# Eight attention units in four lanes ahead of two chunks that run together, and another chain that converts the weights

## The chip, the cores and the metric

The kernel runs on one core of a Trainium2 chip. The time is device microseconds of one execution; of the kernel before there are three: 1543.84, 1540.35 and 1537.54 us, median 1540.35 us. The engines are TensorE (PE, its weight loads PEld), VectorE (DVE), ScalarE (ACT), GpSimd (POOL) and SyncE (SP), which here only issues DMA transfers. Each engine runs its own instructions in the order in which they stand in its program.

## The reference, cut to what is computed

```
def sm_attn(qq, kk, vv):                      # scale = 1/8
    s = scale * qq @ kk.T
    a = exp(s - max(s));  a = a / (sum(a) + 1e-09)
    return a @ vv
# 8 batches, 8 heads, 576 positions, head width 64, 32 packed queries p
p_packed = sm_attn(p, k, v)
x = sm_attn(q, p_packed, p_packed)            # as (8, 576, 512)
# first mixer
x_prev = x moved by one position
xk = mu_k*x + (1-mu_k)*x_prev;  xr = mu_r*x + (1-mu_r)*x_prev
x2 = sigmoid(xr @ w_r) * (relu(xk @ w_k)**2 @ w_v)      # 512 -> 1024 -> 512
# second mixer
u = x2 + (U, V of rank 32 over the positions)
out = u + relu(u @ w_ch1) @ w_ch2                       # 512 -> 2048 -> 512
```

The weights come as 64-bit floats, q, k, v and p as 32-bit floats.

## The kernel before

**Units and chunks.** Attention is cut into 16 units: batch pair b (0 to 3) times head pair j (0 to 3), unit u = 4b + j. `attention_steps` computes one: it transposes k on PE, forms the packed scores, takes exp, transposes q and the weights, forms the packed output `pp`, the second scores, a second softmax (`a2`, `s2`: 20 groups of 32 columns) and the output `xo`, which one DMA writes to `x_d`. Every product goes through a PSUM tile `psat`, and ACT or DVE copies it out. A unit loads three inputs `kin`, `qin`, `vin` of 576 KB each.

The first mixer works on 12 chunks of 384 positions, three to a batch pair. Chunk n reads x of all four units of its batch pair, mixes it (`mix`, tiles `xr` and `xk`, each in two halves hi and lo), then `r_block` (three of 12 products, PSUM `psr`), `k_block` (eight of 12 products, `psk`, then relu, square and split to `kk`), `v_block` (eight of 9 products into three accumulators `psv`), `x2_out` and `xu_block`. The second mixer (`psc`) begins when all chunks are done.

**Weights.** `Cast.run` loads 128x512 64-bit words into `st` and makes from the two 32-bit halves of each a hi and a lo tile (fp32r). The four tiles of w_r and the left half of w_k (`wk_0`) are needed for a chunk's start, the right half (`wk_1`) from its fifth `k_block` on, the eight of w_v (`wv`) in its `v_block`s. The first eight conversions stand between the first loads (`FIRST`), the other twelve behind them. The 34 conversions of V, w_ch1 and w_ch2 follow during the chunks. `st` has 2 buffers, and the scratch tiles `a` and `m` have 2 each.

**Order of the work.** `Plan` collects all operations with a class and a sequence number, and `emit` walks through them with its own costs and writes the engines' programs; a `copy` goes to ACT or DVE as it falls out there. So the order within each engine is fixed when the program is built. At the start units 0 to 3 run together in four lanes (buffer sets A, B, C, D: `AX_`), each `LAG` = 3 steps behind the one before, with all eight PSUM banks. Lane A has eight big buffers and loads unit 4's inputs while unit 0 runs; B, C and D have four each, and their memory then becomes `w1b` (wk_1 and wv) and the chunk pools (`open_c`). After that chunk 0 begins, and units 4 to 15 follow one at a time in lane A with two PSUM banks, their steps lying between the chunks' products: units 4 to 7 from chunk 0 on, since chunk 3 needs them, 8 to 11 from chunk 3, 12 to 15 from chunk 6.

## Time and profile before

| | |
|---|---|
| median of three runs | 1540.35 us (1537.54 to 1543.84) |
| profiled execution | span 1538.1 us from its first to its last instruction; the profile names no other time of it |
| busy share of the span | PE 97%, PEld 85%, DVE 63%, ACT 46%, POOL 18% |
| mean granted TensorE clock | 0.984 of 2.4 GHz |
| chain that ended last | PE 91%, DMA 3%, DVE 2%, SP 2%, ACT 2% |

The profiled execution's span lies 2.25 us under the median of the runs, and within their spread. A busy PE is not a PE at its peak: a product at half clock, or one that waits inside the pipeline, counts as busy too. In the chain that ended last a run of products on PE shows how long they take when nothing is in their way.

### The profile page before, as it was taken

What the parts mean: (1) busy time and instruction counts of PE and PEld (TensorE: products, weight loads), DVE (VectorE), ACT (ScalarE), POOL (GpSimd) and SP (SyncE); (2) the same over time, 40 slices, a digit from 0 to 9 for tenths busy, and PEclk for the clock granted to TensorE, in tenths of its full rate; (3) what the DMA queues carried; (4) which work ended last, traced back from release to release, by engine and by line L of the source; (5) the groups of instructions that cost most, each with busy time, mean ns of one, the idle gap of its engine ahead of it and who ended that gap; (6) DMA issues with size and microseconds to landing.
All of it is one profiled execution on the core that took longest, in us unless ns stands there. A gap on an engine that the chain in (4) does not pass through costs nothing.

```text
span 1538.1 us, 25958 instructions
## 1 busy us (share of the span) xinstructions
PE 1491.3 (97%) x9460; PEld 1303.1 (85%) x9460; DVE 962.4 (63%) x2221; ACT 707.1 (46%) x1635; POOL 270.3 (18%) x522
## 2 busy tenths in 40 slices
PE   6779899999999999999999999999999999999998
PEld 4657688888888888888899999999999899999997
DVE  6888877888778886875745454444535354444533
ACT  5777657656756765665522232323222232322221
POOL 0000000000000000001233333333333333333331
PEclk9779999999999999999999999999999999999999
DMA  9865455555555444656877767686866767676763
GB/s 232 206 156 147 122 141 159 155 165 153 160 149 154 139 152 144 223 206 209 263 178 217 190 172 221 166 239 160 230 165 188 203 166 225 161 219 157 205 170 101
DMA packets 202174, 275.67 MB, mean 179 GB/s; under 512 B 68928, under 2 KB 95872, under 8 KB 202048
## 3 DMA queue, kind: packets, MB, share of 16 engines
q0 software_dynamic: 72576, 132.15, 33.0%
q1 hardware_dynamic: 129472, 141.87, 31.1%
q8 instruction: 76, 1.25, 0.3%
q14 instruction: 50, 0.41, 0.1%
HBM read 221.45 MB, written 52.50 MB: 178 GB/s over the span
## 4 chain that ended last, share of the span: by engine, by line
PE 91%; DMA 3%; DVE 2%; SPq 2%; ACT 2%; issue 1%; DVEq 0%
PE psc L197 49%; PE psk L197 13%; PE psv L197 13%; PE psr L197 6%; PE psat L197 4%; PE psat L209 2%; SPq L312 2%; PE psu L197 1%; PE psh L197 1%; PE pst L209 1%; DMA vin<-in_v_dram 1%; DMA s<-w_d 1%; DMA st<-in_moe_w_k_dram 0%; ACT a L230 0%; DMA kin<-in_k_dram 0%
## 5 line engine op out<-in xcount | busy, mean ns | idle before, releaser
L197 PE MATMUL psc<-w,hid 128*128 128x512 f32 x1728 | 446.2, 393 | 1.3 <-ACT xu L281 1.3
L197 PEld LDWEIGHTS psc<-ob,wb 128*128 128x128 f32 x3024 | 406.9, 190 | 26.7
L197 PE MATMUL psc<-ob,wb 128*128 128x256 f32 x3024 | 420.8, 283 | 0.0
L312 POOL DMA_DIRECT2D wb<-ws_d x504 | 267.2, 531 | 593.6 <-PE psc L197 498.6
L197 PEld LDWEIGHTS psc<-w,hid 128*128 128x128 f32 x1728 | 306.2, 189 | 52.0 <-ACT xu L281 1.6
L197 PE MATMUL psk<-xk,wk 128*128 128x384 f32 x1152 | 232.3, 344 | 3.4 <-ACT sq L230 2.4
L197 PE MATMUL psv<-wv,kk 128*128 128x512 f32 x864 | 231.7, 402 | 3.7 <-DVE wv L251 2.2
L197 PEld LDWEIGHTS psk<-xk,wk 128*128 128x128 f32 x1152 | 202.4, 189 | 13.9 <-ACT sq L230 3.3
L251 DVE TENSOR_TENSOR tmp<-tmp,psc 128x256 f32<-128x256 f32 x288 | 120.5, 419 | 143.4 <-PE psc L197 142.2
L230 ACT ACTIVATE hid<-tmp 128x256 fp32r<-128x256 f32 x216 | 85.2, 417 | 262.9 <-DVE tmp L251 262.7
L197 PEld LDWEIGHTS psv<-wv,kk 128*128 128x128 f32 x864 | 157.4, 189 | 37.9 <-DVE wv L251 4.2
L266 DVE SCALAR_TENSOR_TENSOR hid<-psc,hid 128x256 fp32r<-128x256 f32 x72 | 30.5, 424 | 188.3 <-ACT hid L230 188.3
L197 PE MATMUL psr<-wr,xr 128*128 128x512 f32 x432 | 114.7, 408 | 6.9 <-ACT r L281 2.7
L281 ACT ACTIVATE tmp<-psc 128x256 f32<-128x256 f32 x144 | 54.6, 379 | 126.5 <-PE psc L197 126.5
L197 PEld LDWEIGHTS psr<-wr,xr 128*128 128x128 f32 x432 | 80.7, 193 | 26.5 <-ACT r L281 3.8
L266 DVE SCALAR_TENSOR_TENSOR hid<-tmp,hid 128x256 fp32r<-128x256 f32 x216 | 86.3, 422 | 23.6 <-ACT hid L230 19.1
L304 POOL MEMSET x<- 128x8 f32 x4 | 0.5, 134 | 563.6 <-DVE m L263 385.9
L251 DVE TENSOR_TENSOR kk<-sq,kk 128x384 fp32r<-128x384 f32 x96 | 52.6, 552 | 41.3 <-ACT kk L281 41.1
L230 ACT ACTIVATE sq<-psk 128x384 f32<-128x384 f32 x96 | 46.4, 487 | 67.8 <-PE psk L197 66.9
L230 ACT ACTIVATE hid<-psc 128x256 fp32r<-128x256 f32 x72 | 27.5, 382 | 102.6 <-PE psc L197 102.6
L263 DVE SCALAR_TENSOR_TENSOR m<-x,mu_t,m 128x384 f32<-128x384 f32 x96 | 57.8, 611 | 6.6 <-ACT m L230 6.4
L230 ACT ACTIVATE m<-x,om_t 128x384 f32<-128x384 f32 x96 | 57.3, 610 | 7.5 <-DVE xk L251 3.8
(152 smaller groups left out, 1670.4 us busy)
## 6 DMA issues: line engine op xcount, KB each, us to landing
wb<-ws_d POOLq DMA_DIRECT2D x504, 256.0 KB, 3.1
st<-in_moe_w_ch_dram SPq DMA_DIRECT2D x32, 512.0 KB, 4.3
ws_d<-wb SPq DMA_DIRECT2D x56, 256.0 KB, 3.2
...
```

Source lines behind the costliest of these rows:

```text
L197: self.nc.tensor.matmul(o, l, r, start=start, stop=stop, **k)
L209: self.nc.tensor.transpose(out.get(), in_.get(), ident.get())
L230: self.nc.scalar.activation(o, in_.get(), func, **k)
L251: return self.elem(engs, lambda e, o, x, y: e.tensor_tensor(out=o, in0=x, in1=y, op=op), out, [a, b], self.TT, cls)
L263: ("dve",), lambda e, o, x, y, z: e.scalar_tensor_tensor(out=o, in0=x, scalar=z, in1=y, op0=op0, op1=op1), out, [a, b, s], {"dve": (1.042, ...
L266: ("dve",), lambda e, o, x, y: e.scalar_tensor_tensor(out=o, in0=x, scalar=s, in1=y, op0=op0, op1=op1), out, [a, b], self.TT, cls)
L281: self.nc.scalar.activation(o, i, AF.Copy)
L304: (self.nc.gpsimd if eng == "pool" else self.nc.vector).memset(o, 0.0)
L312: (self.nc.sync if eng == "sp" else self.nc.gpsimd).dma_start(out=o, in_=i)
```

## The change

Units 0 to 7 run first, two after another in each of the four lanes (`ORDER`). In lanes B, C and D the second unit's buffers are claimed, and its loads issued, only where the first one makes `xo`. Once unit 3 is done attention leaves PSUM banks 3 and 4 to `psr` and `psk`. Chunks 0 and 1 then go together: their mixes and `r_block`s are in class 0, as attention is, their `k_block`s and `v_block`s alternate, and chunk 1 has three more accumulators, in banks 5 to 7. Lane A's eight big buffers serve meanwhile as `rs` (six r tiles), `x_lead` and `kk_lead` (named `prs`). Units 8 to 11 are given with chunk 2, units 12 to 15 with chunk 5. The twelve late conversions write to `w1b`, which opens when all units of lanes B, C and D are done. `st` and the `m` pool get a third buffer, unit 7 is computed in the plain way of units 0 to 6 (`NPLAIN`).

The conversion chain has one ACT operation less (the copy `m`), and on DVE seven operations as before: four tensor_scalar and three scalar_tensor_tensor, where two tensor_scalar, two scalar_tensor_tensor and three tensor_tensor stood; the copy to hi stays, on ACT or DVE. The second softmax of a unit is taken over all 20 groups at once from exp on.

```diff
     LAG = 3
+    LANES, ORDER = "BCD", (0, 1, 2, 3, 0, 1, 2, 3)
+    EARLY = ()
+    LATER = "v0 v1 v2 k0 k1 k2 k3 v3 v4 v5 v6 v7"
+    NLEAD = 2 * NJ
     FIRST = "k0 p0 q0 w0 k1 v0 w1 q1 v1 w2 k2 q2 w3 v2 k3 w4 q3 v3 w5 w6 w7"
-    NPLAIN = 7
+    NPLAIN = 8
...
-        if u_next is not None:
+        def claim():
             A.kin[u_next], A.qin[u_next], A.vin[u_next] = [A.tile_in(n) for n in ("kin", "qin", "vin")]
+
+        early = u_next is not None and not A.first
+        if early:
+            claim()
...
-        if u_next is not None:
+        if early:
             A.load_k(u_next, A.after)
 
...
-        plan.reduce(st[:, 0:1], sps[0][:, 0:320], ALU.max)
-        plan.reduce(st[:, 1:2], sps[1][:, 0:256], ALU.max)
-        plan.tt(st[:, 2:3], st[:, 0:1], st[:, 1:2], ALU.max)
-        plan.ts(st[:, 3:4], st[:, 2:3], -SCALE, None, mul)
+        s0, s1 = st.at(0), st.at(1)
+        plan.reduce(s0[:, 0:1], sps[0][:, 0:320], ALU.max)
+        plan.reduce(s0[:, 1:2], sps[1][:, 0:256], ALU.max)
+        plan.ts(s0[:, 3:4], s0[:, 0:1], s0[:, 1:2], -SCALE, ALU.max, mul)
...
-            av, s = a2.on(g)[:, g0:g1, :], s2.at(g)
-            bc = [P, g1 - g0, NP]
-            plan.reduce(s[:, 0, g0:g1], sv, ALU.max)
-            plan.tt(av, sv, s[:, 0, g0:g1].unsqueeze(2).to_broadcast(bc), sub)
-            plan.act(av, av, AF.Exp, scale=SCALE)
-            plan.reduce(s[:, 1, g0:g1], av, add)
-            plan.ts(s[:, 2, g0:g1], s[:, 1, g0:g1], 1e-9, None, add)
-            plan.recip(s[:, 3, g0:g1], s[:, 2, g0:g1])
-            plan.tt(av, av, s[:, 3, g0:g1].unsqueeze(2).to_broadcast(bc), mul)
-
...
+            plan.reduce(s2.at(g)[:, 0, g0:g1], sv, ALU.max)
+            plan.tt(a2.on(g)[:, g0:g1, :], sv,
+                    s2.at(g)[:, 0, g0:g1].unsqueeze(2).to_broadcast([P, g1 - g0, NP]), sub)
+        plan.act(a2, a2, AF.Exp, scale=SCALE)
+        plan.reduce(s2[:, 1, :], a2, add)
+        plan.ts(s2[:, 2, :], s2[:, 1, :], 1e-9, None, add)
+        plan.recip(s2[:, 3, :], s2[:, 2, :])
+        plan.tt(a2, a2, s2[:, 3, :].unsqueeze(2).to_broadcast([P, 20, NP]), mul)
+
+        a2f = a2g = a2.rearrange("p g k -> p (g k)")
...
+        if u_next is not None and A.first:
+            claim()
+            A.load_k(u_next)
+            A.load_q(u_next)
+            A.load_v(u_next)
...
-            top = h = sv[:, :, 1].bitcast(F32)
+            top, hb, low = sv[:, :, 1].bitcast(F32), sv[:, :, 1], sv[:, :, 0]
+            ab, mb = a.bitcast(I32), m.bitcast(I32)
             plan.act(a, top, AF.Abs)
-            plan.stt(h, a, 1.125 * 2.0 ** -15, top, ALU.is_ge, mul)
-            plan.act(m, sv[:, :, 0].bitcast(U32), AF.Copy, scale=2.0 ** -52)
-            hb, ab = sv[:, :, 1], a.bitcast(I32)
-            plan.ts(ab, hb, 3, 0x3FFFFFF8, ALU.logical_shift_left, ALU.bitwise_and)
-            plan.stt(ab, hb, -0x40000000, ab, ALU.bitwise_and, ALU.bitwise_or)
-            plan.ts(hb, ab, -0x800000, None, ALU.bitwise_and)
-            plan.tt(m, m, h, mul)
-            plan.tt(m, m, a, add)
+            plan.ts(a, a, 1.125 * 2.0 ** -15, None, ALU.max)
             if parts is None:
+                plan.ts(mb, ab, 3, 0x3FFFFFF8, ALU.logical_shift_left, ALU.bitwise_and)
...
+                plan.stt(m, low.bitcast(U32), 2.0 ** -52, top, mul, mul)
+                plan.tt(m, m, a, add)
                 put(whole[1])
             else:
-                split(*parts, m)
+                hi, lo = parts
+                plan.ts(mb, ab, 3, 0x3FFFF000, ALU.logical_shift_left, ALU.bitwise_and)
+                plan.stt(mb, hb, -0x40000000, mb, ALU.bitwise_and, ALU.bitwise_or)
+                plan.copy(hi, m)
+                plan.ts(hb, mb, -0x800000, None, ALU.bitwise_and)
+                plan.ts(ab, ab, 0x1FF, None, ALU.bitwise_and)
+                plan.stt(a, ab, 2.0 ** 32, low.bitcast(U32), mul, add)
+                plan.stt(lo, a, 2.0 ** -52, top, mul, mul)
...
-                                  for n, b in (("xin", 1), ("mix", 6), ("m", 2))]
+                                  for n, b in (("xin", 1), ("mix", 6), ("m", 3))]
...
-    AX_ = [A0] + [Bufs(es_st, n, "left", 4, True) for n in "BCD"]
+    AX_ = [A0] + [Bufs(es_st, n, "left", 4, True) for n in LANES]
+    lane = [AX_[i] for i in ORDER]
+    nxt = {}
+    for u in range(NLEAD):
+        nxt[u] = next((w for w in range(u + 1, NLEAD) if lane[w] is lane[u]), None)
...
-    steps = [attention_steps(AX_[u], u, NJ if u == 0 else None) for u in range(NJ)]
+    steps = [attention_steps(lane[u], u, nxt[u]) for u in range(NLEAD)]
+    prev = {w: u for u, w in nxt.items()}
     step = 0
     while any(s is not None for s in steps):
+        if steps[NJ - 1] is None:
+            att_banks[0] = banks[0:3] + banks[5:8]
         for i, s in enumerate(steps):
-            if s is not None and step >= i * LAG and next(s, False) is False:
+            if s is None or step < i * LAG or (i in prev and steps[prev[i]] is not None):
+                continue
+            if next(s, False) is False:
                 steps[i] = None
         step += 1
     att_banks[0] = ps_a
     A0.after = ()
+    rs = [plan.tile(A0.big_p, [P, 1152], F32, "big", parts=(0, 1), name="rs") for _ in range(3)]
+    r_lead = [t.at(h)[:, h * 512:(h + 1) * 512] for t in rs for h in range(2)]
+    pairs = [plan.tile(A0.big_p, [P, 1152], F32R, "big", parts=(0, 1), name="prs")[:, 0:2 * CW]
+             .rearrange("p (a c) -> p a c", a=2) for _ in range(5)]
+    x_lead, kk_lead = pairs[0:2], pairs[2:5]
+    xin_lead = [t.vt.bitcast(F32)[:, 0:1024].rearrange("p (j c) -> p j c", j=2) for t in kk_lead[1:3]]
 
...
-        cast_v(m)
+    late_casts = LATER.split()
+    for _ in EARLY:
+        cast_late(late_casts.pop(0))
+    plan.open(cpools + [w1b], [pl for A in AX_[1:] for pl in A.pools], open_c)
+    for t in late_casts:
+        cast_late(t)
...
+        if n == 1:
+            for h, t in enumerate(xin_lead):
+                plan.dma(t, x_d[b].rearrange("(j p) n -> p j n", p=P)[:, 2 * h:2 * h + 2, c * CW - P:c * CW + CW], cls=0)
+            xin[n] = lambda j: xin_lead[j // 2][:, j % 2]
+            return
...
-        s = plan.tile(hid_p, [P, CW], F32, "s", name="sq")
+        s = plan.tile(m_p, [P, CW], F32, "m", name="sq")
         plan.act(s, ps[:, 0:CW], AF.Relu)
         plan.square(s, s)
-        kk = plan.tile(kk_p, [P, 2, CW], F32R, "kk", parts=(0, 1))
+        if n < 2 and (2 * m + n) % 6 < 3:
+            kk = kk_lead[(2 * m + n) % 3]
+        else:
+            kk = plan.tile(kk_p, [P, 2, CW], F32R, "kk", parts=(0, 1))
...
-            vps[:] = [plan.bank(ps_v, "psv") for _ in range(3)]
+            vps[n] = [plan.bank(banks[5 + t:6 + t] if n == 1 else ps_v, "psv", n != 1) for t in range(3)]
...
-    CAST0, NPER = 1, 5
+    CAST0, NPER = 2, 5
...
+        return [(n, t, x2_out(n, t)) for t in range(3)]
+
+    plan.cls = 0
+    evac = []
+    for n in range(2):
+        load_x(n)
+        for j in range(NJ):
+            mix(n, 1, j, x_lead[j - 2] if n == 1 and j >= 2 else None)
+        for t in range(3):
+            evac.append(r_block(n, t))
+        for j in range(NJ):
+            mix(n, 0, j, xm[n, 1, j] if n == 1 else None)
+    for n in range(2):
+        sigmoid(n, evac + [x_last[0]])
+    plan.cls = 1
+    load_x(2)
+    for m in range(MK):
+        for n in range(2):
+            k_block(n, m)
+        if m >= 2:
+            for n in range(2):
+                v_block(n, m - 2)
+    for n in range(2):
+        v_block(n, MK - 2)
     for j in range(NJ):
-        mix(0, 1, j)
+        mix(2, 1, j)
     x2s = []
-    for n in range(len(chunks)):
+    A0.load_k(NLEAD)
+    A0.load_q(NLEAD)
+    A0.load_v(NLEAD)
+    for n in range(2, len(chunks)):
         b, c = chunks[n]
-        if c == 0 and b + 1 < NBP:
...
+        if c == 2 and b + 2 < NBP:
             plan.cls = 1 if b == 0 else 0
-            for u in range((b + 1) * NJ, (b + 2) * NJ):
+            for u in range((b + 2) * NJ, (b + 3) * NJ):
                 attention(A0, u, u + 1 if u + 1 < NU else None)
...
-            if t == 0 and n > 0:
+            if t == 0 and n == 2:
+                for n0 in range(2):
+                    v_block(n0, MK - 1)
+                x2s = [(n0, t0, x2_out(n0, t0)) for t0 in range(3) for n0 in range(2)]
+            elif t == 0:
                 x2s = finish(n - 1)
...
-                if n > 0 and m in (1, 2, 3):
-                    xu_block(n - 1, m - 1, x2s.pop(0))
+                if m > 0 and x2s:
+                    xu_block(*x2s.pop(0))
```

How instructions move is shown at three places. First the lead on PE, where `psat<-ident,kin` begins a unit. In the kernel before, unit 4's transposes of k stand ahead of the end of units 2 and 3, and the first `psr` (chunk 0) behind:

```order
L209 MATMUL psat<-ident,kin 64x128 x2
L209 MATMUL psat<-ident,pbd 128x128
L197 MATMUL psat<-th,ppz 128x320 x2
L197 MATMUL psat<-th,ppz 128x256 x2
L197 MATMUL psat<-kh,pT 32x256 x4
L197 MATMUL psat<-kt,pT 32x64 x4
L197 MATMUL psat<-kh,pT 32x256 x4
L209 MATMUL psat<-ident,a_916 128x128 x5
L197 MATMUL psr<-wr_177,xr 128x512 x2
L197 MATMUL psat<-th,ppz 128x320 x2
L197 MATMUL psat<-th,ppz 128x256 x2
L197 MATMUL psr<-wr_177,xr 128x512
```

In the change the same stretch holds the transposes of units 6 and 7 (`kin`) and chunk 0's first `psr`:

```order
L209 MATMUL psat<-ident,kin 64x128 x2
L209 MATMUL psat<-ident,pbd 128x128
L197 MATMUL psat<-vin,at 32x64 x20
L209 MATMUL psat<-ident,kin 128x128 x4
L197 MATMUL psr<-wr_181,xr 128x512 x2
L209 MATMUL psat<-ident,qin 128x128
L209 MATMUL psat<-ident,pp 128x128
L209 MATMUL psat<-ident,qin 128x128 x2
L197 MATMUL psr<-wr_181,xr 128x512
L209 MATMUL psat<-ident,a_160 128x128 x4
L209 MATMUL psat<-ident,kin 128x128 x4
L197 MATMUL psr<-wr_181,xr 128x512 x3
```

So the first products of the chunks stand where four more units have begun, and each next piece of `psr` has pieces of units 4 to 7 ahead of it.

Second, SP's queue at the end of the lead. Before, the loads of the late weights (`st<-in_moe_w_k`, `st<-in_moe_w_v`) stand between the loads and stores of units 0 to 5:

```order
L312 DMA st<-in_moe_w_k_dram 128x1024
L312 DMA x<-x_d_65 128x4x512
L312 DMA st<-in_moe_w_k_dram 128x1024
L312 DMA st<-in_moe_w_v_dram 128x1024
L312 DMA x_d_66<-xo 128x1152
L312 DMA st<-in_moe_w_v_dram 128x1024
L312 DMA kin<-in_k_dram 128x2x256 x2
L312 DMA kin<-in_k_dram 64x2x64 x2
L312 DMA st<-in_moe_w_v_dram 128x1024 x2
```

In the change three of them stand ahead of unit 2's store, and the other nine behind the stores of units 4 to 7 (`x_d_66<-xo`):

```order
L316 DMA x<-x_d_65 128x2x63
L316 DMA prs<-x_d_65 128x2x512
L316 DMA x_d_66<-xo 128x1152
L316 DMA x<-x_d_65 128x4x512
L316 DMA prs<-x_d_65 128x2x512
L316 DMA x_d_66<-xo 128x1152 x3
L316 DMA st<-in_moe_w_k_dram 128x1024 x4
L316 DMA st<-in_moe_w_v_dram 128x1024 x5
L316 DMA st<-in_moe_U_dram 64x576 x2
L316 DMA x<-x_d_66 128x384
L316 DMA x<-x_d_66 128x2x63
```

Third, PE where the two chunks run together. Before, chunk 0 has one `psk` block after another and a `psv` block (`wv`) as soon as its weights are there:

```order
L197 MATMUL psk<-xk,wk_0_184 128x384 x6
L197 MATMUL psk<-xk,wk_0_181 128x384 x3
L197 MATMUL psk<-xk,wk_0_182 128x384 x3
L197 MATMUL psk<-xk,wk_0_183 128x384 x3
L197 MATMUL psk<-xk,wk_0_184 128x384 x2
L209 MATMUL psat<-ident,a_729 128x128 x4
L197 MATMUL psk<-xk,wk_0_184 128x384
L197 MATMUL psv<-wv_1129,kk 128x512 x9
```

In the change eight `psk` blocks on wk_0 (four for each chunk; `xr` and `prs` hold chunk 1's xk) come first, then `psv` on three tiles of w_v, and the first products with wk_1 lie in small pieces between them:

```order
L197 MATMUL psv<-wv_1887,prs 128x512 x18
L197 MATMUL psk<-xk,wk_0_185 128x384 x3
L197 MATMUL psk<-xk,wk_0_186 128x384 x3
L197 MATMUL psk<-xk,wk_0_187 128x384 x3
L197 MATMUL psk<-xk,wk_0_188 128x384 x3
L197 MATMUL psk<-xr,wk_0_185 128x384 x3
L197 MATMUL psk<-xr,wk_0_186 128x384 x3
L197 MATMUL psk<-prs,wk_0_187 128x384 x3
L197 MATMUL psk<-prs,wk_0_188 128x384 x3
L197 MATMUL psv<-wv_1888,prs 128x512 x9
L197 MATMUL psv<-wv_1888,kk 128x512 x9
L197 MATMUL psk<-xk,wk_1_1890 128x384 x2
```

The next `psk` products wait in this order for the four tiles of wk_1, which are among the nine late loads.

## Rows read from the trace of the kernel before

**Rows 1.** The page, parts 1 and 2: busy shares, and 40 slices of the span.

```profile
PE 1491.3 (97%) x9460; PEld 1303.1 (85%) x9460; DVE 962.4 (63%) x2221; ACT 707.1 (46%) x1635; POOL 270.3 (18%) x522
...
PE   6779899999999999999999999999999999999998
...
PEclk9779999999999999999999999999999999999999
```

**Rows 2.** Busy time by stretch: stretch, length, busy us by engine, clock, DMA, GB/s.

```profile
0.00:20.00 20.00, 11.95 (x124) 8.41 (x124) 9.12 (x26) 9.15 (x22) 1.32 (x11) 1.00 0.95 213
20.00:40.00 20.00, 13.10 (x137) 11.02 (x145) 15.91 (x46) 12.91 (x36) 0.00 (x0) 0.83 1.03 245
40.00:60.00 20.00, 16.63 (x177) 13.47 (x164) 17.59 (x48) 16.31 (x50) 0.00 (x0) 0.74 0.55 146
60.00:80.00 20.00, 14.21 (x96) 10.84 (x88) 17.55 (x46) 12.60 (x32) 0.00 (x0) 0.67 0.98 263
80.00:100.00 20.00, 14.54 (x90) 10.08 (x89) 15.62 (x37) 14.29 (x37) 0.00 (x0) 0.76 0.80 167
100.00:120.00 20.00, 17.01 (x80) 15.00 (x79) 16.81 (x40) 14.33 (x28) 0.00 (x0) 0.81 0.31 106
120.00:140.00 20.00, 19.19 (x121) 15.39 (x120) 15.81 (x33) 15.74 (x38) 0.00 (x0) 1.00 0.42 138
140.00:160.00 20.00, 16.42 (x120) 12.45 (x119) 18.45 (x43) 13.33 (x32) 0.00 (x0) 1.00 0.73 191
...
278.00:607.00 329.00, 328.27 (x2148) 278.73 (x2147) 265.21 (x612) 217.71 (x484) 0.31 (x2) 1.00 0.51 153
```

**Rows 3.** The chain that ended last, 215 to 285 us: start, length, what.

```profile
221.90 0.69 PE psr L197 x3
...
239.97 0.47 PE psu L197 x2
...
278.05 2.73 PE psr L197 x12
```

**Rows 4.** The same chain, 560 to 612 us: a chunk without attention.

```profile
564.26 2.72 PE psr L197 x12
...
569.02 5.44 PE psr L197 x24
...
598.85 2.08 PE psv L197 x9
600.94 2.10 PE psk L197 x12
...
607.16 2.72 PE psr L197 x12
```

**Rows 5.** The timeline of SP, 40 to 90 us: the store of unit 3.

```profile
82.57 0.32 SPq L312 DMA_DIRECT2D x_d<-xo  x1
```

**Rows 6.** Groups by line and shape: conversion, mix and softmax on DVE and ACT.

```profile
L263 DVE SCALAR_TENSOR_TENSOR m<-x,mu_t,m 128x384 f32<-128x384 f32 x96 | 57.8, 611 | 6.6 <-ACT m L230 6.4
...
L266 DVE SCALAR_TENSOR_TENSOR a<-st,a 128x512 int32<-128x512 int32 x52 | 35.4, 682 | 0.2
L266 DVE SCALAR_TENSOR_TENSOR st<-a,st 128x512 f32<-128x512 f32 x52 | 35.4, 686 | 7.5 <-ACT a L230 7.2
L251 DVE TENSOR_TENSOR m<-m,a 128x512 f32<-128x512 f32 x52 | 35.3, 682 | 0.2
...
L230 ACT ACTIVATE m<-st 128x512 f32<-128x512 uint32 x52 | 34.5, 671 | 2.8 <-DMA w_d<-m 2.0 <-DVE wv L251 0.6
...
L251 DVE TENSOR_TENSOR xr<-m,xr 128x384 fp32r<-128x384 f32 x48 | 25.8, 551 | 1.9 <-ACT xr L281 1.8
...
L257 DVE TENSOR_SCALAR a<-st 128x512 int32<-128x512 int32 x52 | 21.5, 418 | 0.2
...
L270 DVE TENSOR_REDUCE s<-a 128x16 f32<-128x512 f32 x16 | 10.9, 679 | 3.3 <-ACT a L230 3.3
...
L257 DVE TENSOR_SCALAR st<-st 128x1 f32<-128x1 f32 x32 | 4.6, 145 | 0.1
```

**Rows 7.** SP's loads of late weights: count, ns, first and last start.

```profile
L312 SPq DMA_DIRECT2D st<-in_moe_w_v_dram x8: 328/346/411, 68.2 to 154.5; - x8
...
L312 SPq DMA_DIRECT2D st<-in_moe_w_k_dram x4: 333/340/352, 86.9 to 105.6; - x4
```

**Rows 8.** What SP's queue waited for, 0 to 230 us: total, times, longest.

```profile
SPq L312 <- DVE m L251: 71.2, 16, 16.3
...
SPq L312 <- DMA x_d<-xo: 8.9, 3, 5.6
```

More of the change, by code (lines that the diff above doesn't have):

```diff
@@ L48, in on, with at @@
         return Ref(self.vt, part, self.chain)
+    def at(self, part):
+        return self.on(part)
     def keys(self):
@@ L255, in ts @@
         k = {} if op1 is None else {"op1": op1}
+        if isinstance(s1, Ref):
+            return self.elem(
+                engs, lambda e, o, x, y: e.tensor_scalar(out=o, in0=x, scalar1=y, scalar2=s2, op0=op0, **k),
+                out, [a, s1], self.TC, cls)
         return self.elem(
@@ L571, in __init__ @@
             self.pbd = plan.fixed(one.tile([P, 2, D], F32, name="pbd"))
+            self.st = plan.fixed(one.tile([P, 16], F32, name="st"), (0, 1))
             self.first = first
             self.pools = [self.big_p, self.one]
-            for f in (self.a1, self.pbd):
+            for f in (self.a1, self.pbd, self.st):
                 f.alloc = plan.add((), lambda: None)
@@ L578, in __init__ @@
             plan.zero(self.a1[:, 512:640])
+            plan.ts(self.st.at(1)[:, 7:8], self.a1[:, 512:513], 1e-9, None, add)
             self.kept = None
@@ L670, in attention_steps @@
         plan.copy(pT, ps[:, 2 * P:3 * P].rearrange("p (b c) -> p b c", b=2))
-        if u_next is not None:
+        if early:
             A.load_k(u_next, A.after)
-        st = plan.tile(A.one, [P, 16], F32, "st", parts=(0, 1))
+        st = A.st
         yield
@@ L719, in attention_steps @@
                 plan.copy(qt[:, 1024:1152], ps[:, 2 * P:3 * P])
-        if u_next is not None:
+        if early:
             A.load_q(u_next, A.after)
@@ L747, in attention_steps @@
             plan.tt(ppz[:, 1, :], pp, ppz[:, 0, :], sub)
-        if u_next is not None:
+        if early:
             A.load_v(u_next, A.after)
@@ L980, in load_x, with mix @@
             plan.zero(t.at(2 * NJ)[:, :, 0:P].rearrange("p j (b c) -> p j b c", b=2)[:, :, :, 0:1])
-        xin[n] = t
-    def mix(n, which, j):
-        x = xin[n].on((j, NJ + j, 2 * NJ))
+        xin[n] = lambda j: t.on((j, NJ + j, 2 * NJ))[:, j]
+    def mix(n, which, j, dst=None):
+        x = xin[n](j)
         f = plan.tile(m_p, [P, CW], F32, "m")
-        plan.act(f, x[:, j, 0:CW], AF.Copy, scale=om_t[:, which, j:j + 1])
-        plan.stt(f, x[:, j, P:P + CW], mu_t[:, which, j:j + 1], f, mul, add)
-        dst = plan.tile(mix_p, [P, 2, CW], F32R, "mx", parts=(0, 1), name=("xk", "xr")[which])
+        plan.act(f, x[:, 0:CW], AF.Copy, scale=om_t[:, which, j:j + 1])
+        plan.stt(f, x[:, P:P + CW], mu_t[:, which, j:j + 1], f, mul, add)
+        if dst is None:
+            dst = plan.tile(mix_p, [P, 2, CW], F32R, "mx", parts=(0, 1), name=("xk", "xr")[which])
         xm[n, which, j] = dst
@@ L1002, in r_block @@
                 i += 1
-        r = plan.tile(r_p, [P, 512], F32, "r")
+        r = r_lead.pop(0) if r_lead else plan.tile(r_p, [P, 512], F32, "r")
         rt[n, t] = r
@@ L1336, in packed_attention_moe_mixer_kernel @@
                 load_w2(m)
-    for t, x2 in enumerate(finish(len(chunks) - 1)):
-        xu_block(len(chunks) - 1, t, x2)
-    plan.open(lpools, [hid_p, kk_p], open_l, after=[opened_r])
+    for item in finish(len(chunks) - 1):
+        xu_block(*item)
+    plan.open(lpools, [kk_p], open_l, after=[opened_r])
     ps_c2, ps_c1 = banks[0:3] + banks[5:6], banks[3:5] + banks[6:7]
```

61 lines of the change are left out of this document (28 added, 33 removed).

## The prediction

> **What bounds the kernel now.** I began with the page's busy shares: PE is busy 97% of the span and DVE 63% [rows 1], so PE looks full. Its slices tell the two stages apart: the first five or so are not full, nor is the granted clock in them [rows 1]. The view by stretches makes that finer [rows 2]: from 20 to 120 us PE is busy 13.1 to 17.0 of each 20 us, at a clock of 0.67 to 0.83 (a mix of the levels 2.4 and 1.2 GHz), while DVE is busy 15.6 to 17.6. From 120 us the clock is at 1.00, and from 278 to 607 us PE is busy 328.27 of 329. There only PE's own work sets the time. What can be won lies at the start.
>
> How much is it? A chunk without attention takes 607.16 - 564.26 = 42.9 us [rows 4]. Chunks 3 to 7, from 278.05 [rows 3] to 564.26 [rows 4], take 286.2, so 71.7 more than five times 42.9. That pays for units 8 to 15 less the half of unit 8 that lies before, 7.5 units: 9.6 us of PE time each, switching included. The work ahead of chunk 3 is then 3 x 42.9 + 8.5 x 9.6 = 210 us, and it took 278. Some 68 us are lost at the start, which is the most that the change could bring. The clock's share of it is in the 20 to 120 us rows: their mean is 0.76.
>
> **The change, against one milestone.** Chunk 3's first `psr` starts at 278.05 in the kernel before [rows 3]. Behind that point both programs have the same left: chunks 3 to 11, the second half of unit 8, units 9 to 15, the second mixer. So I work out when the changed kernel gets there, in three terms.
>
> **Term 1, the lead.** DVE first, since it has the highest busy share of the elementwise engines there. Unit 3's store is issued at 82.57 [rows 5]. Up to there DVE was busy 9.12 + 15.91 + 17.59 + 17.55 + about 2.0 = 62.2 us [rows 2]. Eight conversions are in it: two tensor_scalar at 0.42 and five others at 0.685 [rows 6], 4.27 us each, 34.2 together. With some 2 for the first mixes, units 0 to 3 and the start of unit 4 cost 26, about 6.0 a unit. In the change a conversion has four at 0.42 and three at 0.685, 3.74. The new forms (a maximum with a constant, a product of a 32-bit integer with two factors) are not in the trace; I price them as their nearest rows, 0.42 and 0.685, bounded above by 0.685 for each, which would add 1.1 per conversion. A unit loses six small instructions of 0.145 upwards, and three grow by 128 elements (0.13 each by the row of 679 ns for 512) [rows 6]: about 0.6 saved, 5.4 left. The lead holds 8 units (43), 8 conversions (30), the first five instructions of three more (7), 16 mixes at 0.611 + 0.551 [rows 6] (19), and copies of r and hi halves (4): 103 us, 9 of them in the first 20 us. The other 94 at the share of 20 to 80 us (51.05 of 60, 0.85) end at 131, at that of 80 to 140 (48.24 of 60, 0.80) at 137, at the best row (18.45 of 20) at 122 [rows 2]. I take 0.80, as the conversions that filled DVE's gaps are through by some 75 us and chains of single units remain.
>
> Two other floors lie close. PE has 8 x 9.6 + six `psr` blocks of 2.72 + two `psk` blocks of 2.10 [rows 4] = 97 us, at the clock of 0.76 some 128. DMA has 8 units of 1.77 MB, 11 weight tiles of 0.52, 8 outputs of 0.59 and 2.4 of x: 27 MB, at the mean of the first five rows, 207 GB/s [rows 2], 130 us. The new waits are these: in lanes B, C and D the second unit's loads wait for the first unit's buffers; on SP's queue unit 4's store stands ahead of a half of chunk 1's x, and behind that half's mixes wait `psr` and, on PE, the tails of units 6 and 7. Lead: **137 us, 125 to 152**.
>
> **Term 2, chunks 0 and 1.** PE has 14 `psk` blocks of 2.10 left and 14 `psv` blocks of 2.08 [rows 4]: 58.5. The nine late loads stand behind unit 7's store. DVE then finishes three conversions (3), makes four more (15) and splits some six kk (5); with a load and its first steps ahead, the fourth tile of wk_1 is ready some 27 us into this stage. PE has about 25 us until it needs it: 3 us of stall. For the whole stage DVE has 34 for nine conversions, 3, 9 for splits, 9 for mixes, U and copies: 55 us, hidden behind PE by a thin margin. **62 us, 58 to 75**.
>
> **Term 3, chunk 2.** 42.9, one `psv` block more (2.08), three xu blocks more at 0.47 [rows 3], half of unit 8 (5), and 2 to 3 for unit 8's inputs, whose loads wait for buffers that `x2_out` frees: **54, 51 to 58**. The kernel before took 278.05 - 221.90 = 56.2 here [rows 3], with the rest of unit 7 besides.
>
> Sum: 137 + 62 + 54 = 253, against 278: 25 us won, a span of 1513. Against the median of the runs, 2.25 above this span, that is **1515 us**.
>
> Counted at nothing: the lighter conversions during the later chunks (0.26 us less on DVE, one 0.42 for a 0.685, and the 0.67 us copy `m` less on ACT [rows 6], 34 times), because PE's products hide them: DVE is busy 265 and ACT 218 of 329 there [rows 2]; uncovered, they would be worth up to 23. Unit 7's plain products, the third `m` and `st` buffers and the missing pool are nothing on PE either.
>
> **The rivals.** (a) DVE runs through the lead without gaps, as in its best row. The lead ends at 122 to 127 and the time is about 1500 to 1505. For it: three later lanes have no conversions to compete with. Against: no row before 140 us has that share.
>
> (b) PE becomes the bound of the lead at a low clock. At 0.67, the lowest row, the 87 us left after the first 20 take 130, and the lead ends at 150: 1528. For it: PE is idle often in the lead and the granted clock never held 1.00 between 20 and 120 us [rows 2]; a longer lead has more such work. Against: in the stretch of 100 to 120 us, where products came close together, it was 0.81, and 1.00 after. The Trainium skill's page "TensorE: Matmul & The Clock Gate", section "HAM oscillation — how this bites in real kernels", says that a kernel whose bursts of products are parted by waits falls back to the lower clock again and again. By that rule this rival is the likely one, at about 1528; the 20 to 120 us rows agree with it as to the clock, while PE's idle time in them shows that it was not the bound.
>
> (c) The late weights come too slowly, and the change ends slower. The twelve late loads were issued from 68.2 to 154.5 [rows 7], one per 7.8 us, and SP waited 71.2 us, up to 16.3 at once, for the conversions' scratch `m` [rows 8]. The ninth tile is ready after about nine steps and 9 us. At 7.8 that is 79 us, some 18 after PE wants it: a gain of 7, about 1533. At 8.6 a step nothing is won, at 9.6 the kernel is 0.5% slower, at 10.5 it takes about 1556. Against: in the kernel before, DVE had units 4 to 6 beside them; here it has no attention in that stage, a third `st` buffer, and 3.7 us of work per tile.
>
> **How the numbers follow.** Forecast, 1507 to 1523: 0.50. (a) 0.17. (b), 1523 to 1533: 0.17. (c) up to a step of 9.6, or lead and stage both at their upper bounds, so that the time is about the same: 0.10. (c) beyond that: 0.06. The range 1500 to 1533 holds the forecast, (b) and most of (a), 0.8. A measurement of this kernel can tell about 0.5%, 7.7 us, from no change: faster 0.84, same 0.10, slower 0.06.
>
> **What will show it.** Unit 7's store (the eighth `x_d<-xo`) at about 137 us; chunk 2's first `psr` at about 199; chunk 3's at about 253; chunks without attention still 42.9 apart; DVE's share near 0.8 and the clock below 1 until the lead ends; a PE idle of a few us before the first `psk` on wk_1. The prediction is wrong if the second wave of units takes much longer or shorter than the first, if the late weights hold PE for more than 10 us, or if the stretch behind chunk 3 changes its length by more than 5.

## The result and the profile after

The changed kernel takes **1521.4 us** (median, 1520.6 to 1522.0), the kernel before 1539.8 on the same chip: a ratio of 0.9861, 95% interval 0.9838 to 0.9884 (the two medians alone give 0.9881). Forecast: 1515, range 1500 to 1533, faster.

The page of the changed kernel, busy shares and 40 slices [rows 1]:

```profile
PE 1486.8 (98%) x9456; PEld 1300.8 (86%) x9456; DVE 926.4 (61%) x2092; ACT 692.2 (46%) x1595; POOL 269.3 (18%) x522
...
PE   6899999999999999999999999999999999999998
...
PEclk8689999999999999999999999999999999999999
```

DVE has 36 us less to do. PE is full from the third slice on (before, but for one slice, from the fourth), its clock from the fourth slice on, as before. The milestones stand in SP's timeline (columns: start, length, what; two stores, the second is unit 7's, issued at 141.0) and in the chain that ended last, whose two pieces here are the first `psr` of chunks 2 and 3 [rows 3]:

```profile
136.56 4.75 SPq L316 DMA_DIRECT2D x_d<-xo  x2
```

```profile
202.26 2.72 PE psr L197 x12
...
255.82 1.36 PE psr L197 x6
```

| term | forecast | measured |
|---|---|---|
| lead, to unit 7's store | 137 (125 to 152) | 141.0 |
| chunks 0 and 1 | 62 (58 to 75) | 61.3 |
| chunk 2 | 54 (51 to 58) | 53.6 |
| behind chunk 3's first `psr`, against before | 0 | +2.9 |
| span | 1513 | 1518.8 |

The last but one line: 1518.8 - 255.82 = 1263.0 after, 1538.1 - 278.05 = 1260.1 before. By the start of the `psr` records, which later sections use, the stage of chunks 0 and 1 takes 61.1. Of the 22.2 us won by chunk 3, some 3 are given back, all of them between chunk 3 and chunk 8: this stretch takes 289.4 us, 286.2 before. Chunks without attention are 42.9 apart as before.

The lead by stretches (columns as in [rows 2]), first the whole in two parts, then four pieces of 20 us:

```profile
0.00:101.00 101.00, 79.09 (x747) 59.63 (x748) 68.65 (x179) 59.30 (x170) 1.31 (x11) 0.78 1.01 237
101.00:141.00 40.00, 38.37 (x318) 29.52 (x318) 33.81 (x83) 32.76 (x86) 0.00 (x0) 1.00 0.28 97
```

```profile
40.00:60.00 20.00, 15.85 (x179) 11.24 (x177) 15.23 (x40) 14.00 (x43) 0.00 (x0) 0.84 1.00 209
60.00:80.00 20.00, 16.21 (x77) 11.43 (x77) 12.33 (x30) 7.24 (x18) 0.00 (x0) 0.50 1.08 279
80.00:100.00 20.00, 19.05 (x187) 13.67 (x190) 16.05 (x39) 15.29 (x47) 0.00 (x0) 0.84 1.08 241
100.00:120.00 20.00, 18.57 (x247) 14.00 (x244) 19.13 (x51) 18.05 (x53) 0.00 (x0) 1.00 0.41 128
```

The reader is to see two things. DVE's sum is 68.65 + 33.81 = 102.5, against 103 in the forecast. But it doesn't run at one share: 0.68 up to 101 us, while the 16 DMA engines are busy all the time (1.01; in the kernel before 0.55 to 1.03 in the first five rows of [rows 2]), and 0.85 behind. In those 101 us 24 MB come in (101 us at 237 GB/s). Of the four pieces DVE and ACT are idle most from 60 to 80 us, and there PE works at the lower clock (0.50, which is 1.2 GHz).

In the joint stage (chunks 0 and 1) PE loses 2 us between 161 and 181 us, where the forecast had put 3; the second fence is its row in the waits from 141 to 202 us (total, times, longest):

```profile
141.00:161.00 20.00, 20.00 (x106) 18.71 (x106) 13.03 (x29) 15.52 (x29) 0.00 (x0) 1.00 0.31 101
161.00:181.00 20.00, 18.04 (x88) 15.42 (x88) 19.90 (x46) 11.02 (x21) 0.00 (x0) 1.00 0.45 141
181.00:202.00 21.00, 21.00 (x105) 18.77 (x104) 19.61 (x45) 14.97 (x31) 0.00 (x0) 1.00 0.14 40
```

```profile
PE psk L197 <- DVE wk L270: 1.6, 2, 1.0
```

### The profile page after: what moved, and what is told of

Its sections match the earlier page's. It is cut to its first block, busy times and chain, and to the rows that moved or that the text cites. A ratio compares the mean times of both kernels' runs of the same rounds, so it can differ in the third digit from the quotient of the medians.

```text
span 1518.8 us, 25744 instructions
## 1 busy us (share of the span) xinstructions
PE 1486.8 (98%) x9456; PEld 1300.8 (86%) x9456; DVE 926.4 (61%) x2092; ACT 692.2 (46%) x1595; POOL 269.3 (18%) x522
## 4 chain that ended last, share of the span: by engine, by line
PE 92%; DMA 3%; DVE 2%; SPq 1%; ACT 1%; issue 1%; DVEq 0%
PE psc L197 49%; PE psk L197 13%; PE psv L197 13%; PE psr L197 6%; PE psat L197 5%; PE psat L209 3%; DMA qin<-in_q_dram 1%; PE psh L197 1%; PE pst L209 1%; SPq L316 1%; PE psu L197 1%; DMA kin<-in_k_dram 1%; DMA s<-w_d 1%; DMA st<-in_moe_w_r_dram 0%; DMA raw_v<-v_d 0%
## 5 line engine op out<-in xcount | busy, mean ns | idle before, releaser
L197 PE MATMUL psk<-xk,wk 128*128 128x384 f32 x1056 | 210.3, 341 | 2.0 <-DVE wk L270 1.6
L197 PE MATMUL psv<-wv,kk 128*128 128x512 f32 x783 | 205.9, 398 | 0.0
L197 PEld LDWEIGHTS psk<-xk,wk 128*128 128x128 f32 x1056 | 184.2, 188 | 11.1 <-DVE wk L270 2.2
L197 PEld LDWEIGHTS psv<-wv,kk 128*128 128x128 f32 x783 | 143.5, 188 | 29.1 <-issue 1.4
L197 PE MATMUL psr<-wr,xr 128*128 128x512 f32 x414 | 110.9, 401 | 1.4 <-ACT rs L285 0.6
L197 PEld LDWEIGHTS psr<-wr,xr 128*128 128x128 f32 x414 | 75.1, 188 | 19.1 <-ACT rs L285 1.2
L251 DVE TENSOR_TENSOR kk<-sq,kk 128x384 fp32r<-128x384 f32 x87 | 47.9, 553 | 35.9 <-ACT kk L285 35.8
L267 DVE SCALAR_TENSOR_TENSOR m<-x,mu_t,m 128x384 f32<-128x384 f32 x88 | 52.1, 611 | 0.9 <-ACT m L230 0.7
L230 ACT ACTIVATE m<-x,om_t 128x384 f32<-128x384 f32 x88 | 50.6, 607 | 1.5 <-DVE xr L251 0.9
```

What stands on the lines that cost most here:

```text
L197: self.nc.tensor.matmul(o, l, r, start=start, stop=stop, **k)
L230: self.nc.scalar.activation(o, in_.get(), func, **k)
L251: return self.elem(engs, lambda e, o, x, y: e.tensor_tensor(out=o, in0=x, in1=y, op=op), out, [a, b], self.TT, cls)
L267: ("dve",), lambda e, o, x, y, z: e.scalar_tensor_tensor(out=o, in0=x, scalar=z, in1=y, op0=op0, op1=op1), out, [a, b, s], {"dve": (1.042, ...
```

## The experiments

Three questions were open: what sets the lead, what the joint stage is made of, and where the 3 us behind chunk 3 go. Each ratio is against the kernel before, run on the same chip; the changed kernel's is 0.9861. A store time or a stretch is that of one profiled execution. E5 and E10 have the changed kernel's order of instructions as far as the lead goes, and their stores went out at 142.3 and 138.3 instead of 141.0: differences of the lead below some 4 us say nothing.

**E1, the old conversion chain put back.**

```diff
-            plan.ts(a, a, 1.125 * 2.0 ** -15, None, ALU.max)
+            plan.stt(h, a, 1.125 * 2.0 ** -15, top, ALU.is_ge, mul)
+            plan.act(m, sv[:, :, 0].bitcast(U32), AF.Copy, scale=2.0 ** -52)
...
-                plan.stt(m, low.bitcast(U32), 2.0 ** -52, top, mul, mul)
...
```

> The changed kernel with the old conversion chain put back, and nothing else. The new chain is lighter by 0.53 us on DVE and by one 0.67 us copy on ACT for each weight tile. Theory of the prediction (DVE's sum sets the lead): eleven such conversions stand in the lead, 5.8 us of DVE more, at a share of 0.8 some 5 to 7 us; unit 7's store goes out at 146 to 148 us instead of 141.0, the stage of chunks 0 and 1 grows by 0 to 3 us, and the span is 1524 to 1529. Rival (PE at the low clock and the loads set the middle of the lead, DVE has gaps there): the store moves by less than 2 us and the span stays within 1518 to 1522.

Store at 142.9, within the scatter, and DVE's sum up to it was 102.7 us, no more than in the changed kernel: the planner had put other DVE work behind the store. The joint stage took 69.2 us in this execution, span 1527.2; the median of the four runs is 1524.8 and the ratio 0.9868 (0.9852 to 0.9885), no difference from the changed kernel that can be told. The lighter chain is worth nothing to see in the lead. What it is worth in the joint stage stays uncertain, since at its store PE had done some 30 products fewer than the changed kernel at its own, and they come in that stage.

**E2, the second softmax in two halves again.**

```diff
-        plan.act(a2, a2, AF.Exp, scale=SCALE)
-        plan.reduce(s2[:, 1, :], a2, add)
...
-        plan.tt(a2, a2, s2[:, 3, :].unsqueeze(2).to_broadcast([P, 20, NP]), mul)
...
+            plan.act(av, av, AF.Exp, scale=SCALE)
+            plan.reduce(s[:, 1, g0:g1], av, add)
...
+            plan.tt(av, av, s[:, 3, g0:g1].unsqueeze(2).to_broadcast(bc), mul)
...
```

> The changed kernel with the second softmax in two halves again, as in the kernel before. Per unit DVE gets three small instructions more (a sum, an addition and a reciprocal, 0.15 to 0.2 us each) and a product more, about 0.5 us, and ACT one exponential more. Theory of the prediction (DVE's sum sets the lead): 8 x 0.5 us at a share of 0.8, unit 7's store 4 to 6 us later, at 145 to 147. Rival (PE and loads): less than 2 us later. For the stretch from chunk 3's first psr to chunk 8's, 289.4 us in the changed kernel and 286.2 before: if the merged softmax is what lengthened it, it falls to about 286; if it is the order of PE's products (the six last products of half a unit in two groups of three, with psk between), it stays at 288 to 289.5, since only two of eight units have another order here.

Both were wrong on the store: it went out at 134.4, 6.6 us earlier, with 285 DVE instructions up to it instead of 261 and the same sum (102.7). It was seen again in E9 (134.5). The stretch, 288.8, is what the order of PE's products was to leave (table at E5). The ratio, 0.9839 (0.9817 to 0.9860), can't be told from the changed kernel's. DVE had done 72.8 us of its work by 101 us, where the changed kernel had done 68.7, and the rest took 33 us instead of 40.

**E3, the transposes of `kin` twice.**

```diff
-            for n in range(4):
+            for n in tuple(range(4)) * (2 if u < NLEAD else 1):
                 plan.transpose(ps[:, n * P:(n + 1) * P],
```

> The changed kernel with the eight transposes of kin done twice into the same place in each of the first eight units: 64 transposes more on PE, 0.107 us each at full clock and up to 0.21 at half, 7 to 13 us of PE time, all in the lead; nothing else changes. Theory of the prediction (DVE's sum sets the lead, PE has gaps): unit 7's store 0 to 3 us later, at 141 to 144. Rival (PE at the low clock is the bound from 57 to 86 us and from there on it is full): 6 to 13 us later, at 147 to 154. A third way: the added products raise the granted clock between 59 and 86 us, and the store goes out earlier than 141.

Store at 141.1: 64 products more cost nothing, ratio 0.9844 (0.9829 to 0.9859). So PE was not the bound of the lead. DVE's sum up to 141 us was 105.5, 3 us more than in the changed kernel, and that moved nothing either. The third way was half there: the long piece at the lower clock shrank from 27 us (59 to 86) to 14 (70 to 84), and the store did not move.

**E4, fewer transfers in the lead.**

```diff
             t = self.qin[u]
+            if NJ <= u < NLEAD:
+                plan.zero(t)
+                return
```

(and the same for `vin`)

> The changed kernel without the loads of q and v of units 4 to 7, whose tiles GpSimd fills with zeros instead: 4.7 of about 27 MB of the lead's transfers are left out, and with them that part of the attention is not computed from its data (the instructions on PE, DVE and ACT stay). Theory of the prediction (DVE's sum): unit 7's store at 138 to 141, 0 to 3 us earlier. Rival (the loads hold the lead from 57 to 86 us, with 279 GB/s there and PE waiting on kin and qin): 5 to 12 us earlier, at 129 to 136.

Store at 127.9, 13.1 us earlier, ratio 0.9807 (0.9784 to 0.9831). Its lead in two parts:

```profile
0.00:75.00 75.00, 54.69 (x575) 42.64 (x576) 56.23 (x148) 48.53 (x145) 8.65 (x18) 0.88 0.91 232
75.00:128.00 53.00, 50.95 (x462) 37.46 (x461) 44.62 (x107) 38.58 (x104) 1.07 (x1) 0.95 0.31 107
```

The bulk of the transfers is through some 26 us sooner, and half of that comes back, since DVE has 44.6 us left behind them instead of 33.8, done at the same 0.84. Both leads have these two parts: DVE at a lower share as long as transfers come (0.68, here 0.75), and at 0.84 behind. A load that is left out also no longer waits for its buffers or holds its place on SP's queue, so this run shows what these loads cost the lead, and not that it was their bytes alone.

**E6, the first late loads held back** by an ordering behind the last `vin` load of units 4 to 7 (the same is added for `w_k`).

```diff
-            cast_rows(wv[i], w_v[i * P:(i + 1) * P, :])
+            cast_rows(wv[i], w_v[i * P:(i + 1) * P, :], tuple(v_in[u] for u in range(NJ, NLEAD)))
```

> The changed kernel with the first three w_v loads (1.6 MB, issued at 75 to 80 us) put behind the last vin load of units 5 to 7 on SP's queue. Theory (up to some 100 us the transfers are the bound of the lead, whose DMA share is 0.93 to 1.08 in every 20 us up to there, and the last DVE and PE work follows): the units' last loads land 4 to 6 us earlier, unit 7's store goes out at 134 to 138 instead of 141.0. The stage of chunks 0 and 1 may lose 0 to 3 us again, as its weights come later. Rival (DVE's sum sets the lead): the store stays at 139 to 142.

Store at 139.2, within the scatter, and the joint stage took 62.1; ratio 0.9848 (0.9827 to 0.9870). A miss for the theory: the last `vin` load landed at 96.3, 1.0 us earlier than in the changed kernel (97.3) and not 4 to 6. It was issued no earlier (92.2 for 92.0); between 40 and 97 us SP's queue waited 5.0 us for products of PE, 1.8 in the changed kernel. So the bytes are not all that times the second units' loads; how much is theirs stays open.

**E11, less for DVE in the lead.**

```diff
-        split(dst.at(0)[:, 0, :], dst.at(1)[:, 1, :], f)
+        if n < 2:
+            plan.copy(dst.at(0)[:, 0, :], f)
+            plan.zero(dst.at(1)[:, 1, :].bitcast(F32))
...
```

> The changed kernel in which the 16 low halves of chunks 0 and 1's mixes are filled with zeros by GpSimd instead of being worked out by DVE (0.55 us each, 8.8 us less on DVE in the lead), so that this small part of the mix is left out. Theory of the prediction (DVE's sum at a share sets the lead; in its last 40 us DVE is busy 9 to 10 of 10): unit 7's store 6 to 11 us earlier, at 130 to 135. Rival (the transfers up to 100 us and behind them the chain of the last units set it): 0 to 3 us earlier, at 138 to 141.

Store at 136.0, 5.0 us earlier, between the two: DVE's sum up to it was 97.8, only 4.7 less, as the planner put other work there. The ratio, 0.9879 (0.9862 to 0.9896), shows no gain, and the joint stage says why. Its row in the changed kernel, in E2, in E4 and in E11:

```profile
141.00:202.10 61.10, 59.14 (x296) 52.97 (x296) 52.64 (x117) 41.61 (x80) 0.00 (x0) 1.00 0.29 93
134.40:198.70 64.30, 62.94 (x321) 57.13 (x320) 56.14 (x124) 44.51 (x86) 0.00 (x0) 1.00 0.27 88
127.90:192.80 64.90, 64.12 (x325) 58.01 (x324) 54.62 (x121) 43.85 (x85) 0.00 (x0) 1.00 0.27 87
136.00:200.60 64.60, 63.83 (x323) 57.73 (x323) 52.27 (x116) 42.44 (x83) 1.18 (x3) 1.00 0.27 88
```

Where unit 7's store went out earlier, PE had 25 to 29 products more left for this stage. So chunk 2 began 3.4, 9.3 and 1.5 us earlier, and not 6.6, 13.1 and 5.0: that store is not the end of the lead's work on PE.

**E10, the nine late weight tiles left out.**

```diff
-    for t in late_casts:
-        cast_late(t)
+    for t in late_casts[:3]:
+        cast_late(t)
+    for t in late_casts[3:]:
...
+            plan.zero(w.at(h)[:, h, :].bitcast(F32))
```

> The changed kernel in which the nine late weight tiles (wk_1 and w_v 3 to 7) are filled with zeros by GpSimd at the start of the stage, so that their loads and conversions are left out, and with them that part of the result. Theory (the stage of chunks 0 and 1 is PE's 58.5 us and a stall of 2 to 3 us on late weights): it takes 58 to 59.5 us instead of 61.1. Rival (the rest is not from the late weights): it stays at 60.5 to 62.

The stage took 196.6 - 138.3 = 58.3 us, PE's bare 58.5 of the forecast, and PE waited for nothing. So the late weights, their loads and conversions together, cost the stage 61.1 - 58.3 = 2.8 us, of which PE waits for 2.0.

**E7, the wk_1 tiles first.** `LATER` begins with k0 to k3 instead of v0 to v2.

> The changed kernel with the order of the late weight loads turned: the four wk_1 tiles first, then w_v 0 to 7. Theory of the prediction (a stall of some 3 us before the first psk on wk_1, 2.6 us lost between 161 and 181 us in the trace): that stall goes, w_v 0 comes fourth and may hold its first psv by 0 to 2 us; the stage from unit 7's store to chunk 2's first psr takes 58 to 60 us instead of 61.1. Rival (the rate of the late tiles, one per 4.5 us, holds PE whatever their order): it stays at 60.5 to 64.

61.2 us, the rival's number, but not for its reason. PE's waits in this stage (total, times, longest), and what ACT did ahead of the first:

```profile
PE psk L197 <- ACT sq L230: 1.9, 1, 1.9
PE psk L197 <- DVE wk L270: 0.2, 1, 0.2
```

```profile
144.57 1.28 ACT L230 ACT_TABLE_LOAD   x1
145.87 3.23 ACT L230 ACTIVATE rs<-rs 128x512 f32<-128x512 f32 x6
149.00 0.64 ACT L230 ACTIVATE a<-st 128x512 f32<-128x512 f32 x1
149.55 0.84 ACT L230 ACTIVATE sq<-psk 128x384 f32<-128x384 f32 x2
```

The wait on wk_1 is nearly gone (0.2 for 1.6), as the theory said. The time is lost in another place: PE stands until 150.07 because ACT has the sigmoids of `rs`, with a table load, and the first step of a late conversion in its program ahead of the `sq` that empties a bank of `psk`. The late tiles came at the changed kernel's rate, nine loads from 145.1 to 181.8 us (146.6 to 182.5 there, one per 4.5 us). The ratio 0.9846 (0.9826 to 0.9866) comes with a shorter stretch behind chunk 3, 286.5 (below).

**E12, two buffers for loaded weights** (`bufs=2` for `cvst`).

> The changed kernel with two buffers for loaded weights instead of three. Theory of the prediction (the third buffer counted at nothing; the late tiles come at 4.5 us each because DVE has no attention beside them): the lead and the stage of chunks 0 and 1 change by less than 1.5 us. Rival (the third buffer hides the load, which takes 5 to 7 us to land): the late tiles come at 5.5 to 6.5 us each, the stage takes 67 to 75 us instead of 61.1, and the time is 5 to 13 us longer.

The rival holds: late loads one per 5.65 us (142.1 to 187.3), the stage 69.8 us, ratio 0.9901 (0.9884 to 0.9918). PE loses 5 us in one stretch, and SP's queue waits on DVE for the buffers (136 to 206 us):

```profile
156.00:176.00 20.00, 14.82 (x59) 11.36 (x58) 14.69 (x32) 6.48 (x13) 0.00 (x0) 0.84 0.41 130
```

```profile
PE psk L197 <- ACT wk L285: 4.2, 2, 3.5
```

```profile
SPq L316 <- DVE wv L270: 20.2, 4, 11.0
```

The wait of 3.5 us in the second fence ends at 171.65, and from 170 to 178 us the granted clock is at the lower level:

```profile
170.00:178.00 8.00, 6.09 (x17) 5.09 (x18) 7.92 (x18) 4.11 (x8) 0.00 (x0) 0.50 0.23 85
```

So the slower tiles cost PE time twice, 5.2 us of idle time in the stage (2.0 in the changed kernel) and products at half clock (PE is busy 64.6 us in the stage, 59.1 in the changed kernel). The third buffer, counted at nothing in the forecast, is worth 8.7 us of the stage. It is not worth that to the kernel: with two buffers one late conversion less was in the lead, the store went out at 136.3, 4.7 us earlier, and chunk 2 began 4.0 us later than in the changed kernel (206.1 for 202.1); the ratios are 0.9901 and 0.9861.

**E8, the kernel before with the new chain only.** Its diff is the change's part in `Cast.run`.

> The kernel before with the new conversion chain, and nothing else of the change. Each weight tile costs 0.53 us less on DVE and a 0.67 us copy less on ACT. Theory of the prediction (DVE's sum sets the lead): the last lead store and with it chunk 3's first psr come 4 to 8 us earlier than 278, the time is 0.3 to 0.5% below the kernel before. Rival (the transfers set the first 100 us): 0 to 2 us, a ratio of 0.998 to 1.001. The gain of the change then lies in its order of units and chunks.

1.0015 (0.9998 to 1.0031): no gain. In the profiled execution chunk 3 began at 274.2, 3.7 us earlier than before, and the stretch behind it took 289.6 instead of 286.2: won and given back. Here the loss is not in the products of E5 below, of which 12 had gone ahead of the stretch: `psu` took 12.0 us instead of 8.6, 2.6 of it waiting for `xs` (0.7 before), and `psk` 1.8 more. The planner works out the order of PE's products anew whenever any time moves. E1 and E8 together answer where the change's gain comes from: with the old chain it is all there (0.9868), with the new chain alone there is none, and the merged softmax of E2 is not needed for it either. So it lies in the order of units and chunks and the buffers that go with it, which no run here takes apart further than E12.

**E5, the last products of half a unit as one piece.** A second line of the edit, not shown, lets such a piece ask for its two banks.

```diff
+    def mms(self, items):
+        def fn():
...
+            for out, lhsT, rhs, start, stop in items:
+                o, l, r = out.get(), lhsT.get(), rhs.get()
+                self.nc.tensor.matmul(o, l, r, start=start, stop=stop)
...
+            if not plain:
+                plan.mms([(pss[b2][:, 0:w], ppz[b2 * 64:(b2 + 1) * 64, lh, :], rh[b2 * 64:(b2 + 1) * 64, c0:c1],
+                           n == 0, n + 1 == len(terms))
+                          for n, (lh, rh) in enumerate(terms) for b2 in range(2)])
```

> The changed kernel with the six last products of half a unit (th and tl with ppz, for one half of the columns) put on PE as one piece, for units 8 to 15; everything else is left to the planner. Theory (the 3.2 us given back between chunk 3 and chunk 8 are PE's order: products on rows 0 to 63 and on rows 64 to 127 start 0.004 us apart when they stand side by side, and a lone one between two psk takes 0.34 us): these 96 products, 16.2 us of PE in the changed kernel and 13.5 before, take 8 to 10, the stretch from chunk 3's first psr to chunk 8's falls from 289.4 to 280 to 284 us, and the time by 5 to 9 us. Rival (the given back time comes from attention's waits or from the merged softmax): the stretch stays at 288 to 291, since a whole piece must wait for two free banks and comes later.

Right, and beyond its bounds: stretch 278.7, **1510.2 us, ratio 0.9799** (0.9780 to 0.9818), the fastest of all kernels here. PE's timeline shows why (start, length, what); first the changed kernel, one unit's products with `ppz`:

```profile
258.69 0.41 PE L197 MATMUL psat<-th,ppz 64*128 64x320 f32 x1
259.03 0.97 PE L197 MATMUL psr<-wr,xr 128*128 128x512 f32 x3
259.84 1.09 PE L197 MATMUL psv<-wv,kk 128*128 128x512 f32 x4
260.86 0.41 PE L197 MATMUL psat<-th,ppz 64*128 64x320 f32 x1
260.86 0.55 PE L197 MATMUL psat<-tl,ppz 64*128 64x320 f32 x2
...
263.29 0.38 PE L197 MATMUL psat<-th,ppz 64*128 64x256 f32 x1
263.52 0.27 PE L197 MATMUL psat<-tl,ppz 64*128 64x256 f32 x1
263.63 0.27 PE L197 MATMUL psat<-th,ppz 64*128 64x256 f32 x1
263.83 0.96 PE L197 MATMUL psr<-wr,xr 128*128 128x512 f32 x3
264.72 0.38 PE L197 MATMUL psat<-th,ppz 64*128 64x256 f32 x1
264.95 0.28 PE L197 MATMUL psat<-tl,ppz 64*128 64x256 f32 x1
265.06 0.27 PE L197 MATMUL psat<-th,ppz 64*128 64x256 f32 x1
265.27 0.50 PE L197 MATMUL psr<-wr,xr 128*128 128x512 f32 x1
```

and the same half of 256 columns in E5:

```profile
265.03 0.39 PE L212 MATMUL psat<-th,ppz 64*128 64x256 f32 x2
265.25 0.28 PE L212 MATMUL psat<-tl,ppz 64*128 64x256 f32 x2
265.37 0.28 PE L212 MATMUL psat<-th,ppz 64*128 64x256 f32 x2
265.58 1.19 PE L197 MATMUL psr<-wr,xr 128*128 128x512 f32 x4
```

A unit's last products come in two sorts, on rows 0 to 63 and on rows 64 to 127. Side by side they run together: six take 265.58 - 265.03 = 0.55 us. In two groups of three of one sort they take 263.83 - 263.29 = 0.54 and 265.27 - 264.72 = 0.55. Added up over the stretch from chunk 3 to chunk 8 (from each product's start to the next one's), and counted in PE's order (parted: other products stand between the six):

| kernel | of units 8 to 15, parted in the second half | the 96 products, us | stretch, us |
|---|---|---|---|
| before | 3 | 13.5 | 286.2 |
| E7 | 3 | 13.8 | 286.5 |
| E2 | 6 | 15.4 | 288.8 |
| E1 | 7 | 15.7 | 288.8 |
| E3 | 7 | 15.6 | 290.2 |
| E4 | 7 | 15.7 | 290.1 |
| changed | 8 | 16.2 | 289.4 |
| E5 | 0 | 9.5 | 278.7 |

E6, E10 and E11 are as E4 (7 parted units, 15.7 us, 290.1 or 290.2). Of E5's 10.7 us 6.7 are in the 96 products, 3.1 in the `psk`, `psv` and `psr` around them and 1.3 in `psu`, less 0.3 elsewhere. E12 stands outside the table: 5 parted units, 14.8 us, but 290.9, because its `psu` products took 2.6 us longer than in the changed kernel, 2.2 of it waiting for `xs`.

**E9, E5 and E2 together.**

> The last products in one piece, as in e5, and the second softmax in two halves, as in e2. Theory (e2's store at 134.4 came from the split: its first half's exponential and transposes need not wait for the second half, and chains of single units end the lead): the store goes out at 133 to 137 again, the stretch from chunk 3 to chunk 8 is 278 to 280 as in e5, and the time is 1504 to 1508. Rival (e2's earlier store was scatter of the lead's clock from one execution to the next): the store at 139 to 143, the time 1509 to 1512 as for e5.

The store came at 134.5, so that part of the theory holds, and the stretch took 285.8 instead of 278 to 280: 1513.8 us, ratio 0.9835 (0.9817 to 0.9853), no faster than E5. The 96 products took 9.9; what is new is in PE's waits from chunk 3 on, where E5 had none:

```profile
PE psu L197 <- DVE xs L304: 2.3, 5, 0.5
PE psu L197 <- DVE xs L267: 1.1, 4, 0.4
```

The `psu` products took 12.75 us there, 7.31 in E5. The planner, with other release times, put them where `xs` was not yet ready.

## Why the prediction was right, and where it was off

The milestone argument held: chunk 3 began 22.2 us earlier (25 forecast), and 19.3 of them were left in the span.

**Term 1** came out at 141.0 for 137. DVE's sum was right (102.5 for 103), and the size of the miss is small, but the step "I take 0.80" put one share on a lead that has two: 0.68 while the transfers run and 0.85 behind them. The forecast had the transfers as a floor of its own, 27 MB or 130 us, and passed on; the loads set the first part. Leaving 4.7 MB of them out moved the lead most (E4, -13.1), by their bytes or by their waits (E6). The sum that the runs support is the transfers' end and then what DVE has left at a share of some 0.85: 101 + 33.8 / 0.85 = 141, which restates the measured rows, and in E4 75 + 44.6 / 0.85 = 127 for 127.9. In E2 and E9, 29.5 and 30.2 us were left and took 33 and 33.5; in E12, 31.0 took 35. Why the split softmax lets DVE do more by 101 us was not tried by itself; its chain is shorter, since the first half need not wait for the second, but that is argued and not shown. The store was also not quite the milestone that the sum took it for: an earlier one left PE more work for the next stage (E11).

**Rival (b)**, PE at a low clock. The clock did stay low for 27 us in one piece, lower than the forecast had it there (0.50 against a lowest row of 0.67), yet E3 put 64 more products into the lead for nothing. The Trainium skill's page "TensorE: Matmul & The Clock Gate", section "HAM oscillation — how this bites in real kernels", says that bursts parted by waits for data bring the clock down: the trace agrees as to the clock, 0.50 from 59 to 86 us, with PE waiting 1.2 us for ACT before 58.1 and 1.4 for the load of `qin` before 61.0. The time that the rival drew from it, 1528, did not come.

**Term 2** was right as worked out: 58.5 of products (E10: 58.3) and a stall of 3 (2.8), on wk_1 as forecast (1.6 us of waits). What it did not see is that the stall is not wk_1's alone: with those tiles first PE waits for ACT instead, and the stage is as long (E7). Rival (c) is the stall on late tiles at a slower rate, and E12 shows what kept it away: the third `st` buffer, which the forecast had counted at nothing. At 5.65 us a tile instead of 4.5 the stage takes 8.7 us more.

**Term 3** was right (53.6 for 54).

**Behind chunk 3** the forecast had nothing, since both programs have the same left. The same products, but not in the same order: +2.65 us for the 96 products with `ppz` and +1.0 for the `psk` around them, less 0.4 elsewhere. The table and E5, which takes these losses out, show the mechanism, and that the kernel before had lost some of it too. The lighter conversions in the later chunks are hidden, as forecast: E8 gained nothing, and E1 lost nothing there (288.8).

Of the miss of 5.8 us in the span, 4.0 are the lead, 2.9 the order behind chunk 3, and -1.1 the two terms between.
